# Sixteen hand-written orders of work, each replaced by another, in a gated mix of two recurrent attentions on one core

## The chip, the core and the metric

The kernel runs on one core of one Trainium2 chip. A core has five engines that work side by side, each through its own queue in order: TensorE (PE: matmuls; PEld is its loading of weights), VectorE (DVE), ScalarE (ACT), GpSimd (POOL) and SyncE (SP), which here only issues DMAs. Data lies in SBUF; matmuls write to PSUM, which the kernel uses as eight banks of 128 x 512 float32. The metric is device time in microseconds.

## The reference

`x` is [1, 2048, 512], all inputs bfloat16. Two branches read the same `x` and a gate per row mixes them:

```python
g = sigmoid((x * gate_w).sum(-1, keepdims=True))
return g * a + (1 - g) * b

# branch A: 64 segments of 32 tokens, one after the other; 8 rows of memory go from one to the next
mem = mem0                                           # [1, 8, 512]
for s in range(64):
    h = concatenate([mem, x[:, 32*s:32*s+32]], 1)    # 40 rows
    q, k, v = h @ Wq, h @ Wk, h @ Wv                 # 32 heads of 128: 512 -> 4096 each
    p = softmax(mask(q @ k.T * 128**-0.5))           # 40 x 40 for each head
    o = (p @ v) @ Wo                                 # 4096 -> 512
    mem = o[:, :8];  outs.append(o[:, 8:])

# branch B: 32 heads of 16, four stretches of 512 tokens
for s in range(4):
    a_dot = softmax(q_s @ k_s.T * 0.25 + causal) @ v_s
    a_mem = (phi(q_s) @ M) / (phi(q_s) @ z + 1e-6)   # phi(t) = t + 1 if t > 0 else exp(t)
    out_s = g_B * a_mem + (1 - g_B) * a_dot
    M, z = M + phi(k_s).T @ v_s, z + phi(k_s).sum(rows)
b = concat(out_s) @ wo
```

Branch A is a chain of 64 segments: the first rows of a segment's output are needed before the next segment's projections can begin.

## The kernel before

**Staging.** After some warming matmuls the kernel loads `x`, transposes it on TensorE (xT, features on partitions), and projects three of the four stretches of branch B (keys, queries and values, stored to DRAM scratch, and the sums M and z). The weights of branch A follow on SyncE's queue meanwhile. This takes to about 50 us and is not touched by the change. From there on, `plan_a` works off branch A's 64 segments in 16 groups of four, and the rest of branch B (its local attention, the projections of its fourth stretch, and the output rows) is strewn between.

**A segment.** Its 40 rows are 8 of memory and 32 of tokens. 32 rows (8 of memory and 24 of tokens, `hT`) go through the segment itself; the last 8 token rows of the four segments of a group are gathered into one set of 32 "left" rows (`xL`), which is projected once a group, ahead of its group. Four matmuls with 32 columns of weights each (`128*32`) stand side by side in the array, so a pass of 512 columns fills a whole bank.

**Who sets the order.** There is no scheduler. Each group has a list of unit names, written out in the source (`A_LIST0` to `A_LIST15`). `plan_a` reads it from left to right; each name records the instructions of one unit with what they read and write. Each engine executes its own instructions in the order recorded. The waits follow from the reads and writes: an engine waits at an instruction until what it needs has been done elsewhere. PSUM banks are given out in the same order (`Banks.take`, `give`), so a unit may also wait for the copy that frees its bank. SyncE's DMAs, too, stand in the recorded order, and one that waits holds up all behind it. The trace holds each engine's instructions in this order, so that each can be given its unit's name.

The names: `s.u` is unit u of segment s (0 to 3) of the group.
- `K0x K0y`, `Q1x` ...: a projection of one half of the heads (0, 1) in two half passes of eight matmuls each (L1305); `k0`, `q1`, `v0`: its copy from PSUM, on ScalarE (L390) or VectorE (L392); `TK0`, `TQ0`: the transpose on VectorE (L1317).
- `S0` scores (L1598, L1603), `X0` exp on ScalarE (L1612), `Y0` mask on VectorE (L1616), `M0` sums on TensorE (L1633), `L0` their reciprocal as ln and exp on ScalarE (L1640, L1643), `N0` the normalisation on VectorE (L1647), `n0` that of the left columns on GpSimd (L1653).
- `PV0` P times V (L1663), `PL0` the part with the left rows' values VL (L1675), `E0a E0b` the copies to OT, `W0a` ... four output passes (L1392).
- `H0`, `H1`: copies of the output's two halves to `WF` (L390 or L392); `F0`, `F1`: folds, small float32 matmuls that add the four strips and transpose (L1410); `hm0`, `hm1`: copies of the memory rows to the next segment's `hT`; `ax0`, `ax1`: of the other rows to `aT_st`. `oL`, `xc`, `qt` are copies on GpSimd.
- without a segment: `KL0x KL0 KL0e`, `QL..`, `VL..`: projection of the next group's left rows and its copies (with `i` in front: of group 0's own); once both halves of VL are copied they are stored to scratch (L1340, `scr_vld<-VNL`), and `VLt` loads them back in another arrangement (L1348, four DMAs `VL<-scr_vld`). `ol..`, `of`: the output of the left rows. `tl`, `tb`, `tf` (with `e`: their second part): the output rows of a finished group; `os` stores a group's rows.
- branch B: `bS` scores (L933), `bE` one exp of four (L954, `PT`, with a mask on GpSimd, L960), `bP` P times V (L986), `bT` the rest of a head group on VectorE (L1010 to L1046). `pj`, `pp`: a half pass of the fourth stretch's projections (L837) and its copy, which is followed by a store (L864; `t_sb` for the values). `wl`: one of eight loads of Wo (L552).
- `~` behind a name lets ScalarE and VectorE change places for the copies of this unit.

The functions that turn a name into instructions are the same in both kernels; a few lines fix what a name does with the engines:

```python
for u in ORDERS[g]:
    v.swap = u[-1] == "~"
    u = u.rstrip("~")
    if u in common:
        common[u]()
    elif u[0] in "0123":
        seg[int(u[0])][u[2:]]()
```

## Time and profile before

| | us |
|---|---|
| median of 3 runs | 836.16 (833.71 to 837.33) |
| the profiled execution's own time | 836.46 |
| its span, first to last instruction | 834.7 |
| TensorE busy in the span | 806.3 (97%) |
| ScalarE, VectorE, GpSimd busy | 597.6, 572.2, 285.3 |
| exps of branch B (L954), the largest group | 174.4, 320 of 0.607 |
| passes of 512 columns with Wq, Wk, Wv (L1305 on hT) | 138.3, 136.1, 138.7, 2048 matmuls each |

How to read it: the span lies inside the execution's own time, 1.8 us shorter. A matmul is counted from its start to its modelled end, some 0.38 us for 512 columns, while the next ones are already running; a matmul that starts late by less than that leaves no gap in the busy time. Times within the span are given from its start. The granted clock of TensorE is 1.000 over the span.

### The profile page before, as it was taken

The numbers are of one execution on the slowest core, as the hardware profiler recorded it, in microseconds if no ns is written. First come the engines' busy times: TensorE is split into PE (matmuls) and PEld (weight loads), VectorE is DVE, ScalarE is ACT, GpSimd is POOL, SyncE is SP. The second block draws the span as 40 slices with busy tenths as digits, with TensorE's granted clock in tenths as the row PEclk, the third lists the DMA queues.
The fourth block names the chain that finished last, engine by engine and source line by source line (L and its number), as shares of the span: only waits on it lengthen the run. The fifth ranks groups of instructions, "written<-read, shape, count | busy, mean of one in ns | idle before, by whom it ended". The sixth has DMA issues, their size and how long they took to land.

```text
span 834.7 us, 49033 instructions
## 1 busy us (share of the span) xinstructions
PE 806.3 (97%) x21947; PEld 433.9 (52%) x21947; DVE 572.2 (69%) x1379; ACT 597.6 (72%) x1523; POOL 285.3 (34%) x780
## 2 busy tenths in 40 slices
PE   9998999999999999999999999999999999999998
PEld 4644455555555555555555555554555554555544
DVE  4555565577677777777776776777776777777664
ACT  5546777777776777777677787777778676778645
POOL 3603242333333333334242333333333233434111
PEclk9999999999999999999999999999999999999999
DMA  8997312112111111111101121111112112110121
GB/s 327 418 370 224 81 32 67 42 32 47 33 30 40 31 48 29 44 39 46 36 20 40 36 56 26 46 39 34 36 32 53 22 37 46 44 38 5 29 60 41
DMA packets 98257, 57.48 MB, mean 69 GB/s; under 512 B 71800, under 2 KB 92160, under 8 KB 96512
## 3 DMA queue, kind: packets, MB, share of 16 engines
q1 hardware_dynamic: 97488, 53.58, 22.1%
q8 instruction: 172, 2.82, 1.4%
q10 hardware_dynamic: 560, 0.79, 0.3%
q14 instruction: 37, 0.30, 0.1%
HBM read 37.14 MB, written 17.20 MB: 65 GB/s over the span
## 4 chain that ended last, share of the span: by engine, by line
PE 82%; ACT 8%; DVE 4%; DMA 3%; issue 1%; SPq 1%; POOL 0%; ACTq 0%; DVEq 0%
PE ps L1305 45%; PE ps L1392 16%; PE ps L1410 3%; PE ps L1663 3%; PE ps L933 2%; PE ps L986 2%; DMA scr_kqd<-stgk 2%; PE ps L1598 1%; PE ps L699 1%; PE ps L1505 1%; PE ps L1633 1%; ACT PT L954 1%; ACT R_sb L1643 1%; ACT WF L390 1%; DVE P_sb L1647 1%
## 5 line engine op out<-in xcount | busy, mean ns | idle before, releaser
L960 POOL TENSOR_SCALAR_AFFINE_SELECT PT<-PT 128x128 bf16<-128x128 bf16 (+2 forms) x320 | 117.2, 366 | 197.4 <-ACT PT L954 156.8
L954 ACT ACTIVATE PT<-ps 128x512 bf16<-128x512 f32 x320 | 174.4, 607 | 3.8 <-PE ps L986 2.1
L1305 PE MATMUL ps<-Wq_sb,hT 128*32 128x512 bf16 x2048 | 138.3, 379 | 1.7 <-ACT PT L954 0.9
L1305 PE MATMUL ps<-Wv_sb,hT 128*32 128x512 bf16 x2048 | 138.7, 379 | 0.0
L1305 PE MATMUL ps<-Wk_sb,hT 128*32 128x512 bf16 x2048 | 136.1, 379 | 0.4
L1392 PE MATMUL ps<-Wo_sb,OT_sb 128*32 128x512 bf16 x2048 | 129.5, 380 | 0.7 <-ACT OT_sb L390 0.6
L1653 POOL TENSOR_TENSOR P_sb<-P_sb,R_sb 128x64 bf16<-128x64 bf16 x128 | 50.7, 396 | 145.3 <-ACT R_sb L1643 136.9
L390 ACT ACTIVATE OT_sb<-ps 128x320 bf16<-128x320 f32 x167 | 67.0, 434 | 24.2 <-PE ps L1675 22.9
L1305 PEld LDWEIGHTS ps<-Wq_sb,hT 128*32 128x32 bf16 x2048 | 58.7, 97 | 48.3 <-ACT hT L390 4.5
L1305 PEld LDWEIGHTS ps<-Wk_sb,hT 128*32 128x32 bf16 x2048 | 59.1, 97 | 45.4 <-ACT hT L390 2.1
L390 ACT ACTIVATE WF<-ps 128x256 f32<-128x256 f32 x108 | 36.2, 381 | 55.5 <-PE ps L1392 53.3
L1317 DVE STREAM_TRANSPOSE QT_sb<-QN_sb 128x256 f32<-128x256 f32 x128 | 56.2, 440 | 26.6 <-ACT QN_sb L390 24.3
L1317 DVE STREAM_TRANSPOSE KT_sb<-KN_sb 128x256 f32<-128x256 f32 x128 | 55.8, 438 | 24.6 <-ACT KN_sb L390 22.0
L390 ACT ACTIVATE QN_sb<-ps 128x512 bf16<-128x512 f32 x85 | 51.0, 600 | 29.8 <-PE ps L1305 28.5
L1392 PEld LDWEIGHTS ps<-Wo_sb,OT_sb 128*32 128x32 bf16 x2048 | 47.3, 96 | 46.0 <-ACT OT_sb L390 7.9
L390 ACT ACTIVATE KN_sb<-ps 128x512 bf16<-128x512 f32 x82 | 49.3, 601 | 29.2 <-PE ps L1305 28.7
L1305 PEld LDWEIGHTS ps<-Wv_sb,hT 128*32 128x32 bf16 x2048 | 50.4, 95 | 27.1 <-ACT QN_sb L390 0.7
L1612 ACT ACTIVATE P_sb<-ps 128x224 bf16<-128x224 f32 x128 | 45.8, 360 | 24.3 <-PE ps L1603 14.0
L1647 DVE TENSOR_TENSOR P_sb<-P_sb,R_sb 128x160 bf16<-128x160 bf16 x128 | 42.8, 335 | 22.4 <-ACT R_sb L1643 21.2
L392 DVE CAST OT_sb<-ps 128x320 bf16<-128x320 f32 x89 | 42.1, 487 | 19.0 <-PE ps L1675 18.1
L392 DVE CAST V_sb<-ps 128x512 bf16<-128x512 f32 x75 | 51.0, 681 | 4.2 <-PE ps L1305 2.5
L1663 PEld LDWEIGHTS ps<-P_sb,V_sb 32*128 32x128 bf16 x2048 | 23.2, 91 | 57.3 <-DVE P_sb L1647 21.8
(139 smaller groups left out, 1480.5 us busy)
## 6 DMA issues: line engine op xcount, KB each, us to landing
Wk_sb<-in_A_Wk_dram SPq DMA_DIRECT2D x4, 1024.0 KB, 10.2
Wq_sb<-in_A_Wq_dram SPq DMA_DIRECT2D x4, 1024.0 KB, 13.7
Wv_sb<-in_A_Wv_dram SPq DMA_DIRECT2D x4, 1024.0 KB, 16.0
Wo_sb<-in_A_Wo_dram SPq DMA_DIRECT2D x8, 512.0 KB, 5.3
scr_vld<-VNL SPq DMA_DIRECT2D x16, 256.0 KB, 3.3
VL<-scr_vld SPq DMA_DIRECT2D x64, 64.0 KB
scr_kqd<-stgk SPq DMA_DIRECT2D x12, 256.0 KB, 9.8
Vj<-scr_vd SPq DMA_DIRECT2D x32, 68.0 KB, 2.4
```

The source lines that it names most:

```text
L390: P.op("act", lambda a: a.activation(dst, src, ACT.Copy), reads=[v.rbank[k] for k in bks], writes=dres, name=name)
L392: P.op("dve", lambda d: d.tensor_copy(dst, src), reads=[v.rbank[k] for k in bks], writes=dres, name=name)
L954: P.op("act", lambda a: a.activation(pt, v.pb[bk], ACT.Exp, scale=v.SCALE_B), reads=[v.rbank[bk]], writes=[rp], name="be%d_%d" % (n, t))
L960: P.op("gp", lambda g: g.affine_select(mv, mv, [[0, len(cut)], [1, 128]], ALU.is_ge, 0.0, base=0, channel_multiplier=-1), reads=[rp], writ ...
L1305: ins = pe.matmul(pb[bk][SEG * j:SEG * (j + 1), :], lhs(c), cols(w, j) if split else w[:, 512 * j:512 * (j + 1)], start=(c == 0), stop=(c ...
L1317: P.op("dve", lambda d: d.transpose(to, src), reads=reads, writes=writes, name=name)
L1392: ins = pe.matmul(pb[bk][SEG * j:SEG * (j + 1), :], lhs(4 * k + j), Wo_sb[:, 4 * k + j, :], start=(first and k == ks[0]), stop=False, skip ...
L1410: ins = pe.matmul(pb[bk][SEG * j:SEG * (j + 1), SEG * n:SEG * (n + 1)], cols, v.fold[:, :], start=True, stop=True, skip_group_check=True)
L1612: P.op("act", lambda a: a.activation(P_sb[:, b, :], pb[bk][:, 0:224], ACT.Exp, scale=SCALE), reads=[rbank[bk]], writes=[Rs("P%d" % b), Rs( ...
L1647: P.op("dve", lambda d: d.tensor_tensor(wide(P_sb, b)[:, :, 0:L], wide(P_sb, b)[:, :, 0:L], R_sb[:, b, :].rearrange("p (i q) -> p i q", q= ...
L1653: P.op(ENG["n"], lambda d: d.tensor_tensor(left(P_sb), left(P_sb), grp04(R_sb[:, b, :]), ALU.mult), reads=[Rs("R%d" % b)], writes=[Rs("P%d ...
L1663: ins = pe.matmul(pb[bks[j]][:, L * i:L * (i + 1)], V_sb[SEG * j:SEG * (j + 1), b, i * E:(i + 1) * E], P_sb[SEG * j:SEG * (j + 1), b, LW * ...
```

## The change

All sixteen lists are replaced by other orders of the same units; nothing else is changed. Both kernels record 2337 groups of matmuls, 20667 matmuls, 776 instructions on GpSimd and 493 DMAs on SyncE. The places of `~` are other ones too: 1509 activations on ScalarE instead of 1522, and 485 copies on VectorE instead of 472. Of the copies to WF 31 instead of 20 are VectorE's. The instructions up to the last sums of branch B's third stretch, at 50 us, are the same, and then hardly two units in a row. The first list's beginning and the end of the last one, as a diff (lines left out of each list are marked):

```diff
 A_LIST0 = """
-    wl ixl iQL0x iKL0x 0.Q1x 0.Q1y iKL0 iKL0e~ wl iQL0 iQL0e~ 0.Q0x 0.Q0y iQL1x iQL1 0.K0x 0.K0y 0.k0 iQL1e pj 0.q1 wl iKL1x iKL1 iKL1e~ bS bE 0.V0x 0.q0
-    iVL0x 0.TQ0 0.V0y 0.V1x pj 0.V1y iVL0 0.TK0 pj pp 0.v1 bE 0.qt bE iVL0e~ pj bE iVL1x iVL1 xl bS iVL1e bP 0.xc bP QL0x bE bE 0.TQ1 0.v0 0.S0 wl 0.K1x
-    0.K1y KL1x bE wl 0.X0 0.Y0 bE KL1 pj pp 0.k1~ KL1e wl iVLt wl 0.TK1 0.M0 0.L0 QL0 bP wl QL0e bS 0.N0 bP bE VL0x VL0 0.S1 1.qt bE 0.X1 bE QL1x 0.Y1
-    VL0e QL1 pj pp QL1e~ 0.M1 0.L1 KL0x KL0 0.n0 0.n1 VL1x VL1 bE 0.PV0 0.PL0 0.N1 pj 0.E0a 0.E0b~ KL0e 0.PV1 0.PL1 0.E1b~ 0.E1a VL1e~ pj VLt 0.W0b 0.W0a
-    bP 0.W1a bP pp bT 0.W1b 0.H0 0.H1~ 1.xc bS 0.F0 bE 0.hm0 0.ax0 0.F1 0.hm1~ 1.K0x 0.oL bE 1.Q0x 1.K0y 1.k0~ 1.Q1x 1.Q1y 1.q1~ bE 1.TK0 1.Q0y bE 1.K1x
-    1.K1y bP bP 1.TQ1 1.q0~ 1.TQ0 1.V1x 1.S0 1.k1 1.TK1 1.X0 1.Y0 1.V0x 1.S1 1.X1 1.V0y 1.M0 1.V1y 1.L0 1.Y1 1.M1 1.L1 1.v0 1.n0 1.N0 1.PV0 1.PL0 1.n1
...
+    ixl wl 0.Q0x iKL0x iQL1x iQL0x 0.K0x 0.Q0y iQL0 0.K1x 0.K1y 0.q0 0.TQ0 iKL0 0.xc iQL0e 0.K0y iKL0e~ iKL1x 0.k1 bS wl bE bE bE iQL1 wl bE 0.k0~ iKL1 pj
+    iQL1e 0.qt 0.TK1 iVL1x iVL1 iVL0x iVL0 xl bP iVL0e pj bP iKL1e~ 0.TK0 0.Q1x iVL1e~ QL0x pp QL0 QL0e wl 0.Q1y bS VL0x wl bE VL0 0.V0x wl wl pj iVLt
+    0.q1~ bE 0.S0 bE pj KL1x 0.TQ1 bE 0.X0 0.Y0 0.S1 KL0x 0.X1 0.Y1 bP wl 0.V0y VL0e~ 0.M1 0.v0 bP 0.L1 0.N1 0.M0 KL1 KL0 pp VL1x VL1 KL1e KL0e~ bS 0.n1
+    pj pj 0.L0 0.N0 QL1x QL1 0.n0 VL1e~ bE bE 0.V1x 0.V1y bE QL1e bE 0.v1~ 0.PV0 1.qt 0.PL0 0.E0a 0.E0b~ 1.xc pj bP 0.PV1 0.PL1 0.E1a~ 0.W0b 0.E1b~ 0.W0a
+    0.oL 0.W1a bT 0.W1b pp 0.H0~ bP bS 0.F0 0.H1~ bE 0.hm0 0.ax0 pj 0.F1 0.hm1~ 1.Q0x 1.K0x 1.K0y bE bE 1.k0 0.ax1~ 1.TK0 1.Q0y 1.q0~ 1.TQ0 bE 1.K1x 1.K1y
+    1.Q1x 1.Q1y 1.k1 bP 1.TK1 1.S0 1.q1 1.TQ1 1.X0 1.Y0 1.V0x 1.V0y 1.v0 pp 1.S1 1.X1 1.Y1 1.M0 1.V1x 1.V1y 1.L0 1.n0 2.qt 1.N0 1.M1 1.L1 bP 1.n1 pj 1.v1
...
 A_LIST15 = """
...
-    2.H0 2.H1 2.F0 2.hm0 pl0 2.F1 2.hm1 3.K0x tfe 3.Q0x 2.ax0~ 3.Q0y 3.q0~ 3.K0y 3.k0 3.TQ0 3.K1x 3.K1y 3.Q1x tl 3.Q1y 3.TK0 3.S0 3.V0x 3.k1~ 3.q1 3.TK1
-    3.X0 3.TQ1 pl1x 3.V0y 3.Y0 3.S1 3.M0 2.ax1 3.X1 tb 3.v0 3.Y1 3.L0 3.n0 tbe 3.V1x 3.M1 tf 3.N0 tfe 3.L1 3.n1 3.N1 3.PV0 3.PL0 3.E0b~ 3.E0a 3.V1y 3.v1~
-    pl1 pl1e 3.W0a 3.PV1 3.PL1 3.W0b pf 3.E1b~ 3.W1b 3.E1a pfe~ 3.W1a 3.H0 3.H1 tl tb 3.F0 3.ax0 3.F1 3.ax1 tbe tf tfe
...
+    3.qt 2.F0 2.hm0 pl0 2.F1 3.Q0x 2.hm1~ 3.K0x 3.K0y tfe 3.Q0y 3.K1x 3.K1y 3.k0~ 3.TK0 3.Q1x 3.Q1y 3.q0~ 3.TQ0 2.ax1~ 3.S0 3.V0x 3.k1~ 3.TK1 3.q1 3.TQ1
+    3.V1x 3.V0y tl tf 3.S1 3.X0 3.Y0 3.X1 3.M0 tb 3.V1y 3.v0 3.L0 3.Y1 3.M1 3.N0 3.v1 2.ax0 tbe 3.L1 3.N1 tfe 3.n0 3.n1 3.PV0 3.PL0 3.E0b pl1x pl1 3.PV1
+    3.PL1 3.E1b 3.E0a 3.W0b 3.W0a 3.W1b 3.E1a pl1e 3.W1a 3.H0 pf pfe 3.H1 tl tb 3.F0 3.ax0~ 3.F1 tbe 3.ax1 tf tfe
     """
```

In group 0, for example, the old order begins with passes of the left rows and of Q1, has `bS` behind `0.K0y`, the four half passes of `iVL` spread over the units from `0.V0x` to `iVL1`, and `iVLt` behind the sixth `wl`; the new one begins with `0.Q0x`, has `bS` earlier, the four half passes of `iVL` in a row and `iVLt` behind the seventh `wl`. In the last group both end with the folds of segment 63, the left rows' output and the last output rows.

## The prediction

> **What bounds the kernel now.** I read the page first, then the table of stretches, then who TensorE waited for, and last the timeline of TensorE and of the DMA queue in the stretch after 50 us.

> ```profile
> span 834.7 us, 49033 instructions
> ...
> PE 806.3 (97%) x21947; PEld 433.9 (52%) x21947; DVE 572.2 (69%) x1379; ACT 597.6 (72%) x1523; POOL 285.3 (34%) x780
> ...
> PEclk9999999999999999999999999999999999999999
> ```

> TensorE is the bound from end to end, at the full granted clock; ScalarE and VectorE have a quarter of their time free. An order of units can only win or lose TensorE's waiting time. The table of stretches (span, TensorE, its weight loads, VectorE, ScalarE, GpSimd, clock, DMA share, GB/s) says where that is densest:

> ```profile
> 50.00:80.00 30.00, 26.15 (x597) 12.50 (x597) 16.64 (x36) 16.84 (x38) 7.55 (x21) 1.00 0.91 291
> 80.00:110.00 30.00, 28.51 (x816) 15.23 (x812) 17.65 (x44) 22.61 (x58) 9.39 (x27) 1.00 0.31 74
> 510.00:610.00 100.00, 98.88 (x2816) 51.89 (x2802) 74.34 (x179) 73.94 (x195) 35.21 (x90) 1.00 0.15 36
> ```

> From 50 to 80 us TensorE is idle 13% of the time, with the DMA engines 91% busy; later it is 1 to 3%. Its waits by releaser (total, times, longest):

> ```profile
> PE ps L1663 <- DVE P_sb L1647: 6.2, 16, 0.7
> PE ps L1410 <- ACT WF L390: 3.1, 13, 1.0
> ...
> PE ps L1675 <- DMA VL<-scr_vld: 1.2, 1, 1.2
> ```

> P times V waits for the normalisation (L1647), the folds wait for the copies of WF, and once the values of the left rows come late by DMA. These gaps count only what exceeds a matmul's own latency. A finer measure: the trace keeps the program's order, so each group of matmuls can be named by its unit, and the time from a group's start to the next can be set against the shortest usual one for that pair of kinds. A half pass of eight matmuls of 512 columns takes 0.43 us (50.49 to 50.92 on the timeline), scores 0.15, sums 0.10, P times V 0.10 plus 0.12, one fold 0.12; the step from a pass into P times V or into the local scores costs 0.54 instead of 0.43. So summed, all groups after 49.75 us need 727.2 us packed. The last group starts at 831.40, so 54.4 us are lost to waits: 5.3 up to the first pass of segment 1 at 79.75 us, and 49.1 in the 752 us behind it (0.78 a segment).

> The three largest early losses are on TensorE's timeline (start, length, group, idle time and its releaser):

> ```profile
> 62.84 0.40 PE L933 MATMUL ps<-QTj,KTj 32*128 32x256 bf16 x8 [0.89 <-ACT PT L954]
> ...
> 73.80 0.21 PE L1675 MATMUL ps<-P_sb,VL 32*128 32x64 bf16 x4 [1.16 <-DMA VL<-scr_vld]
> ...
> 79.07 0.33 PE L1410 MATMUL ps<-fold,WF 128*32 128x32 f32 x16 [1.00 <-ACT WF L390]
> ```

> and the DMA queue in front of the second:

> ```profile
> 62.72 0.34 SPq L1340 DMA_DIRECT2D scr_vld<-VNL  x1
> ...
> 66.52 0.34 SPq L864 DMA_DIRECT2D scr_vd<-t_sb  x1
> 66.90 0.44 SPq L552 DMA_DIRECT2D Wo_sb<-in_A_Wo_dram  x1
> 67.38 3.95 SPq L1348 DMA_DIRECT2D VL<-scr_vld  x4
> ```

> The store of the left values leaves at 62.72, the queue then stands behind the late store of 66.52, and the four loads need 3.95 us to be issued, so the last lands near 73.7.

> **The change, part by part.** Nothing is removed or added: 2337 matmul groups and 493 DMAs on SyncE's queue, before and after. 13 copies go from ScalarE to VectorE (about 13 x 0.6 = 8 us less on an engine busy 598 us, 13 x 0.7 = 9 more on one busy 572): free as load, since neither is the bound, and priced below where they stand on a path. *Packed sum:* 727.2 us again; the steps into P times V from something else go from 123 to 126 (3 x 0.11 = +0.3), into the local scores they stay 80. Cost nil.

> *Group 0 up to the first pass of segment 1.* Packed, this stretch is 24.7 us in both. I followed the new order by hand with durations of rows (copies 0.60 on ScalarE, 0.68 on VectorE, transposes 0.44, exp of the local attention every 0.48). Both start at 50.05.
> - The first local scores come earlier, packed at 55.3. They need a bank that the copy of KL0 frees, and it waits for the transpose of QL0, which VectorE reaches after the MZ product (ends 53.4), a copy and two transposes, at 55.0; the copy ends at 55.7. Wait 0.4.
> - The four half passes of VL0 end at 59.1 instead of 61.8, so their store leaves near 59.9, not 62.7. On the queue follow the first late store (60.9, as before: its copy waits for a memset that ended near 60.2) and four Wo loads of 0.46; the value loads need the store's landing, 59.9 + 3.3 = 63.2, then 3.95 to issue and 2.4 to land: 69.6. Their reader is packed at 71.2: the 1.3 us wait goes, with 1.6 us to spare. The last Wo load leaves at 67.5 and lands near 72.1 (72.5 and 77.1 before), ahead of its pass at 73.7.
> - The second local scores, packed at 61.6, need the late copy at 60.9: the 0.9 us wait goes.
> - Smaller: 0.15 at the third local scores (copy of KL1), 0.1 and 0.2 at the two P times V (exps and copies on ScalarE end at 71.1 and 72.1).
> - The first fold, 1.0 late before because the ScalarE copy of WF stood behind a late copy that waited for a store, now has its WF copy on VectorE, behind the chain of the local output (0.71 + 0.26 + 0.48): done at 75.0, 0.4 late.

> Waits 1.3 instead of 5.3: **-4.0 us**. Bounds: -5.3 if none is left, +0.8 if the landing goes wrong (a rival below).

> *The rest, 49.1 us of waits.* For each group that waits on another engine I took how much packed TensorE work lies between the last group that this engine had to see and the waiting group, and the mean loss at that distance in the trace of before; the new order has its own counts of such places:
> - fold 0: up to 0.35 us of cover 13 -> 12 (0.28 us lost each), to 0.55 8 -> 10 (0.11)
> - fold 1: up to 0.35 3 -> 5 (0.37), to 0.55 10 -> 5 (0.24), to 0.75 15 -> 18 (0.14)
> - first pass behind a fold: up to 0.13 17 -> 14 (0.24), to 0.35 11 -> 14 (0.20)
> - P times V: up to 0.35 6 -> 5 (0.56), to 0.72 15 -> 15 (0.12)
> - output pass behind its copy: up to 0.45 7 -> 5 (0.23)

> Together -1.3; with classes of 0.1 us the same count gives -2.8. I take **-1.5**, nearer the coarse one, whose classes hold more places. Each place scatters by about its mean: some 120 places by 0.25 us give 2.7 us for one order and 3.9 for the difference of two; that is the bound, from -5.4 to +2.4.

> *WF copies on VectorE.* The second half's go from 15 to 23, the first half's from 5 to 8. In the trace a fold 1 behind VectorE lost 0.16 us, behind ScalarE 0.09: 8 x 0.08 = +0.6; fold 0 lost 0.06 and 0.10: 3 x -0.05 = -0.1. **+0.5**. Queued behind such a copy on VectorE are the memory rows and the copies of the next K and Q; the fold, and through it the next segment, waits for it. Bounds: -0.5, and 11 x 1.1 = +12.1 if each stands behind one VectorE copy and one transpose (0.68 + 0.44).

> *Last group.* The last folds to the last transposition are packed the same (0.9 us); the load for output rows 14 is now nearer its reader, 1.8 instead of 3.6 us in the order, but the queue is free to issue it once the rows before have been stored, near 3 us ahead of VectorE's turn. Nil. *Row stores against the copies that reuse their tile:* within 5 us of cover 3 places before, one of which cost 0.4 us (465.59), and 3 after. Nil.

> **Sum:** -4.0 - 1.5 + 0.5 = -5.0, on the profiled execution's 836.46 (span 834.7 and 1.8 around it): **831.5 us**. The median of the runs shown, 836.16, is 0.3 lower than that execution; against it this is -0.56%.

> [...] The longest gap in TensorE's rows is 1.4 us (start to start at 72.37) and the granted clock is 1.00 in every stretch. [...]

> **The rivals.**
> - *The value loads land late all the same.* If the store takes as long to land as those to the same queue's scr_kqd (9.8 us median, with the DMA engines 91% busy as here), the loads are issued from 69.7 to 73.6 and land at 76.0, a wait of 4.8 us at L1675. The early gain turns to +0.8: 836.46 + 0.8 - 1.0 = 836.3. Against it: this very store had 3.3. It decides from a landing of about 5 us. [...] Chance 0.10.
> - *The early gain is given back later.* Early units pulled forward leave the rest as it was or up to 2.4 us worse, plus the 0.5: 836.46 - 4.0 + 2.9 = 835.4. For it: the packed sum and the counts are nearly the same. Chance 0.20.
> - *Slower: WF copies stand in VectorE's queue.* The segment's recurrence passes through WF, fold and memory rows; eleven more of its WF copies are VectorE's. If each waits for one copy and one transpose, +12.1: 836.46 - 4.0 + 12.1 = 844.6. From 0.4 us a boundary the change loses, from 0.7 by more than a measurement can tell. Against it: the 20 such copies of before lost 0.06 to 0.16 us each. Chance 0.15.

> **How the numbers follow.** Forecast 0.55, of which 0.46 lie under 832.0. What a measurement of this kernel can tell from no change is about 0.5%, 4.2 us: the three runs shown spread by 3.6. Faster by more than that 0.46; within it 0.09 + 0.20 + 0.10 = 0.39; slower 0.15. The range, from 827 (early waits gone entirely and most of the -5.4 behind them) to 838.5 (short of the slower case, past the late landing), leaves out some 0.05 below and 0.14 above.

> **What would show it.** In the profile after: no L1675 wait for VL at the first P times V, with the store of VNL near 60 us; the first fold near 75 us and the first pass of segment 1 near 75.8 instead of 79.75; TensorE busy about 27.5 of the 30 us from 50 to 80; the waits of L1663 on L1647 at or under 6.2 us, of L1410 on WF near 3. Wrong would be a first fold past 78 us, a wait for VL of more than 2 us, or more than 5 us of waits of L1410 on VectorE's WF.

## The result, and the profile after

The changed kernel takes 832.67 us (median of 22 executions, 829.88 to 836.26), the kernel before, beside it on the same chip, 835.46 us (22 executions, 833.61 to 838.33): a ratio of 0.9965, 95% interval 0.9952 to 0.9977. That is 2.8 us less, a real gain, but below the half per cent that was set as the bound for "faster". A second series, taken later, gave 0.9966 (0.9951 to 0.9980).

The profiled execution of the changed kernel took 830.58 us (span 828.9). Against the 836.46 us of the execution profiled before that is 5.9 us, twice what the medians differ by: one lies 2.1 us under its median, the other 1.0 over. So the two traces alone would overstate the gain.

From the page after, and its table of stretches (columns as before: stretch, span, TensorE, weight loads, VectorE, ScalarE, GpSimd, clock, DMA share, GB/s):

```profile
span 828.9 us, 49046 instructions
...
PE 804.7 (97%) x21947; PEld 433.6 (52%) x21947; DVE 575.6 (69%) x1392; ACT 592.2 (71%) x1510; POOL 287.6 (35%) x780
```

```profile
50.00:80.00 30.00, 26.91 (x626) 13.20 (x628) 16.27 (x38) 17.91 (x39) 8.53 (x23) 1.00 0.91 291
80.00:110.00 30.00, 28.95 (x832) 14.59 (x824) 19.69 (x48) 22.84 (x57) 8.58 (x25) 1.00 0.29 73
```

TensorE works 0.8 us more than before in the stretch from 50 to 80, where 1.35 more was forecast (27.5). Its waits after (total, times, longest):

```profile
PE ps L1663 <- DVE P_sb L1647: 2.9, 9, 0.7
PE ps L1410 <- ACT WF L390: 2.2, 11, 0.5
PE ps L1675 <- DMA VL<-scr_vld: 1.9, 1, 1.9
```

P times V and the folds wait less than before (6.2 and 3.1), but the wait on the left values, which was to go, has grown from 1.2 to 1.9 us. TensorE's timeline after shows the early losses:

```profile
55.93 0.40 PE L933 MATMUL ps<-QTj,KTj 32*128 32x256 bf16 x8 [0.56 <-ACT KN_sb L390]
68.76 0.40 PE L933 MATMUL ps<-QTj,KTj 32*128 32x128 bf16 x12 [0.52 <-ACT LN_sb L390]
73.97 0.21 PE L1675 MATMUL ps<-P_sb,VL 32*128 32x64 bf16 x4 [1.90 <-DMA VL<-scr_vld]
```

The chain of waits after, from 55 to 74 us (start, length, what), tells why the third line is there:

```profile
56.03 4.12 DMA scr_mzd<-MZ
...
60.24 0.70 DVE VNL L392
...
61.42 5.09 DMA scr_vld<-VNL
...
68.58 5.26 DMA VL<-scr_vld
...
73.97 0.21 PE ps L1675 x4
```

The half passes of VL0 ended at 59.5, as forecast (59.1). But the copies into VNL started at 60.24, when a store of MZ had landed. The code explains it: the helper that gives each tile the waits of the memory it reuses goes by the first letters of the name, and takes "VNL0" for a part of "VN", the values in V_sb, whose memory held MZ before. VNL has memory of its own. In the kernel before the copies came at 61.68, behind that landing, and the false wait cost nothing. The store then took 5.1 us to land, where 3.9 had been enough in the trace of before. The last value load landed 5.3 us after the start of its issue and 4.6 after the end; by the second count the trace of before has 2.3. Loads of Wo, of 512 KB each, stand close in front of both: three in front of the store, and four more in front of the value loads. The DMA engines are 91% busy from 50 to 80 us, in both traces.

By the same measure as in the prediction (start to start of the groups less the shortest usual step), TensorE loses 3.8 us instead of 5.3 up to the first pass of segment 1, and 45.1 instead of 49.4 behind it; the packed sums are equal (727.0).

### The profile page after: what moved, and what is told of

It reads as the page before. It is cut to its first block, busy times and chain, and to the rows that moved or that the text cites. A ratio compares the mean times of both kernels' runs of the same rounds, so it can differ in the third digit from the quotient of the medians.

```text
span 828.9 us, 49046 instructions
## 1 busy us (share of the span) xinstructions
PE 804.7 (97%) x21947; PEld 433.6 (52%) x21947; DVE 575.6 (69%) x1392; ACT 592.2 (71%) x1510; POOL 287.6 (35%) x780
## 4 chain that ended last, share of the span: by engine, by line
PE 81%; ACT 7%; DMA 5%; DVE 3%; issue 1%; POOL 1%; SPq 0%; ACTq 0%; DVEq 0%; POOLq 0%
PE ps L1305 44%; PE ps L1392 17%; PE ps L1410 4%; PE ps L1663 3%; PE ps L933 2%; PE ps L986 2%; DMA scr_mzd<-MZ 2%; PE ps L1505 2%; DMA scr_kqd<-stgk 2%; PE ps L1598 2%; PE ps L1633 1%; ACT PT L954 1%; PE ps L699 1%; ACT R_sb L1643 1%; ACT WF L390 1%
## 5 line engine op out<-in xcount | busy, mean ns | idle before, releaser
L954 ACT ACTIVATE PT<-ps 128x512 bf16<-128x512 f32 x320 | 176.1, 609 | 5.8 <-PE ps L933 3.9
L1392 PE MATMUL ps<-Wo_sb,OT_sb 128*32 128x512 bf16 x2048 | 127.4, 380 | 0.0
L390 ACT ACTIVATE OT_sb<-ps 128x320 bf16<-128x320 f32 x167 | 67.9, 434 | 22.8 <-PE ps L1675 21.7
L1392 PEld LDWEIGHTS ps<-Wo_sb,OT_sb 128*32 128x32 bf16 x2048 | 48.1, 96 | 45.7 <-ACT OT_sb L390 6.4
L390 ACT ACTIVATE QN_sb<-ps 128x512 bf16<-128x512 f32 x83 | 49.9, 602 | 28.4 <-PE ps L1305 27.5
L390 ACT ACTIVATE WF<-ps 128x256 f32<-128x256 f32 x97 | 32.8, 381 | 51.6 <-PE ps L1392 51.5
L390 ACT ACTIVATE KN_sb<-ps 128x512 bf16<-128x512 f32 x79 | 47.0, 599 | 25.7 <-PE ps L1305 24.8
L392 DVE CAST V_sb<-ps 128x512 bf16<-128x512 f32 x82 | 55.9, 683 | 4.0 <-PE ps L1305 3.1
L1647 DVE TENSOR_TENSOR P_sb<-P_sb,R_sb 128x160 bf16<-128x160 bf16 x128 | 42.2, 329 | 20.1 <-ACT R_sb L1643 18.4
L1663 PEld LDWEIGHTS ps<-P_sb,V_sb 32*128 32x128 bf16 x2048 | 23.0, 91 | 54.4 <-DVE P_sb L1647 27.9
```

The source lines that it names most:

```text
L390: P.op("act", lambda a: a.activation(dst, src, ACT.Copy), reads=[v.rbank[k] for k in bks], writes=dres, name=name)
L392: P.op("dve", lambda d: d.tensor_copy(dst, src), reads=[v.rbank[k] for k in bks], writes=dres, name=name)
L954: P.op("act", lambda a: a.activation(pt, v.pb[bk], ACT.Exp, scale=v.SCALE_B), reads=[v.rbank[bk]], writes=[rp], name="be%d_%d" % (n, t))
L1392: ins = pe.matmul(pb[bk][SEG * j:SEG * (j + 1), :], lhs(4 * k + j), Wo_sb[:, 4 * k + j, :], start=(first and k == ks[0]), stop=False, skip ...
L1647: P.op("dve", lambda d: d.tensor_tensor(wide(P_sb, b)[:, :, 0:L], wide(P_sb, b)[:, :, 0:L], R_sb[:, b, :].rearrange("p (i q) -> p i q", q= ...
L1663: ins = pe.matmul(pb[bks[j]][:, L * i:L * (i + 1)], V_sb[SEG * j:SEG * (j + 1), b, i * E:(i + 1) * E], P_sb[SEG * j:SEG * (j + 1), b, LW * ...
```

## The experiments

All ratios are to runs of the kernel before on the same chip, with 95% intervals.

**The first list alone, and the other fifteen alone.**

The first run, against the kernel before; the second changes the other fifteen lists in the same way and leaves list 0:

```diff
 A_LIST0 = """
-    wl ixl iQL0x iKL0x 0.Q1x 0.Q1y iKL0 iKL0e~ wl iQL0 iQL0e~ 0.Q0x 0.Q0y iQL1x iQL1 0.K0x 0.K0y 0.k0 iQL1e pj 0.q1 wl iKL1x iKL1 iKL1e~ bS bE 0.V0x 0.q0
+    ixl wl 0.Q0x iKL0x iQL1x iQL0x 0.K0x 0.Q0y iQL0 0.K1x 0.K1y 0.q0 0.TQ0 iKL0 0.xc iQL0e 0.K0y iKL0e~ iKL1x 0.k1 bS wl bE bE bE iQL1 wl bE 0.k0~ iKL1 pj
...
 A_LIST1 = """
-    0.K0x 0.Q0x bE bE 0.Q0y 0.q0 0.TQ0 0.K0y 0.k0 0.Q1x 0.Q1y 0.q1 0.TK0 0.qt 0.TQ1 0.K1x 0.K1y 0.k1 bP bP 0.S0 bT xl KL1x bS 0.X0 0.Y0 0.V0x 0.TK1 KL1
+    pp 0.K0x 0.Q0x bE bE 0.Q0y 0.q0 0.TQ0 0.K0y 0.k0 0.Q1x 0.Q1y 0.q1 0.TK0 0.qt 0.TQ1 0.K1x 0.K1y 0.k1 bP bP 0.S0 bT xl KL1x bS 0.X0 0.Y0 0.V0x 0.TK1 KL1
```

> The new list of group 0 with the old lists of groups 1 to 15 (one no-op finishing step is put ahead of list 1, so that the counts come out). Theory of the prediction: the early waits go, about 4.0 us less than the kernel before. Theory from the trace of the changed kernel: only 1.5 us are gained up to the first pass of segment 1 and 1.7 by the end of group 0, so 1.7 us less, with the wait for VL near 1.9 us in front of the first P times V as in the changed kernel. If the old lists behind it give the head start back: 0 to 0.5 us less.

> The old list of group 0 with the new lists of groups 1 to 15 (one finishing step left out of list 1, the counterpart of the run beside it). Theory of the prediction: -1.5 of waits and +0.5 for the WF copies, 1.0 us less than the kernel before. Theory from the two traces, whose lags behind group 0 differ by 4.1: 4.1 us less. Rival: what the two single traces show beyond the medians is scatter of executions, so 1.1 us less (2.8 in the medians, less 1.7 of group 0).

Measured: the first list alone 836.72 against 837.22, ratio 0.9996 (0.9981 to 1.0011); the rest alone 836.39, 0.9991 (0.9975 to 1.0007). Neither differs from no change; an early gain of 4.0 is excluded, and so is a gain of 4.1 in the rest. The two medians add up to 1.3 us less, the whole change to 2.8; the intervals are too wide to tell whether the two parts help each other. The trace of the first run shows something that none of the expectations had. Its timeline, and its table of stretches:

```profile
74.48 0.23 PE L1675 MATMUL ps<-P_sb,VL 32*128 32x64 bf16 x4 [2.48 <-DMA VL<-scr_vld]
...
76.13 2.79 PE L1392 MATMUL ps<-Wo_sb,OT_sb 128*32 128x512 bf16 x32
```

```profile
74.00:76.00 2.00, 1.52 (x40) 0.76 (x40) 0.49 (x1) 0.44 (x1) 0.00 (x0) 0.64 0.57 198
76.00:78.00 2.00, 2.00 (x40) 0.83 (x32) 1.68 (x4) 0.95 (x2) 0.40 (x1) 0.51 0.29 47
78.00:80.00 2.00, 1.90 (x60) 0.93 (x52) 0.93 (x3) 0.58 (x3) 0.00 (x0) 1.00 0.21 71
```

Behind the wait of 2.5 us the granted clock is at one half, from 74.55 to 77.97 us, and the 32 matmuls of the output passes take 2.79 us where the changed kernel's profiled run, at full clock, took 1.91. The first pass of segment 1 starts at 80.17, at a loss of 5.3 us, as large as before the change. So the longer wait and the clock take back the early gain. Every execution reports its mean granted clock, this profiled one 0.998 over its span: one such stretch takes 0.002 from the mean (half of 3.4 us in 835.4). Ten of the 12 executions of the first run had 0.998 or less, one of the 12 of the second.

**VNL without the false wait.**

```diff
     def late_home(name):
-        if name.startswith(("aTd", "aTg", "PT")):
+        if name.startswith(("aTd", "aTg", "PT", "VNL")):
             return None
```

> The changed kernel, and the tile VNL no longer inherits the waits of V_sb, whose memory it does not share: its copies need not wait until the store of MZ has landed. Theory that this wait is why the early gain is 1.5 and not 4.0: the copies start near 59.2 instead of 60.2, their store leaves near 60.0 instead of 61.4, the Wo loads behind it end 1.4 earlier too, the value loads are issued from 65.1 instead of 66.5, the wait of the first P times V on VL falls from 1.9 to about 0.5 us, and the kernel gains 1.0 to 1.4 us on the changed one. Rival, that the landing is set by the crowded DMA engines: VL lands near 73.9 all the same, wait 1.7 to 1.9, no gain. Second rival: the wait goes but the time is lost at the next late step before segment 1 (first fold still near 77), under 0.4 us gained.

Measured: 833.69, ratio 0.9958 (0.9943 to 0.9972). The copies start at 58.82 and 59.55, the store leaves at 60.74, the loads from 65.64, VL is read at 73.16 instead of 73.97. The false wait was real, and it was worth 0.8 us of landing. The wait on VL is 1.7 (TensorE also arrives 0.5 earlier), the loss up to segment 1 is 2.7 us. The gain of the ratio over the changed kernel, 0.0007, is inside the intervals. So the false wait is a part of the lateness; the rest lies behind the store's issue, with 4.9 us to that of the loads and 7.5 more until VL is read.

**The WF copies on their old engines, in the new order; and the new engines in the old order.**

The first run, at 14 such places, and the second line at 3 such places (list 14 is shown):

```diff
-    0.oL 0.W1a bT 0.W1b pp 0.H0~ bP bS 0.F0 0.H1~ bE 0.hm0 0.ax0 pj 0.F1 0.hm1~ 1.Q0x 1.K0x 1.K0y bE bE 1.k0 0.ax1~ 1.TK0 1.Q0y 1.q0~ 1.TQ0 bE 1.K1x 1.K1y
+    0.oL 0.W1a bT 0.W1b pp 0.H0 bP bS 0.F0 0.H1~ bE 0.hm0 0.ax0 pj 0.F1 0.hm1~ 1.Q0x 1.K0x 1.K0y bE bE 1.k0 0.ax1~ 1.TK0 1.Q0y 1.q0~ 1.TQ0 bE 1.K1x 1.K1y
...
-    2.L1 2.PV0 2.PL0 2.v1 2.E0b 2.E0a~ 2.N1 QL0 ol0x 2.PV1 2.n1 2.PL1 2.W0a 2.W0b 2.E1a~ 2.W1a 2.E1b~ 2.W1b ol0 VLt bP 2.H0 bP QL0e~ 2.F0 2.H1 2.hm0 ol1x
+    2.L1 2.PV0 2.PL0 2.v1 2.E0b 2.E0a~ 2.N1 QL0 ol0x 2.PV1 2.n1 2.PL1 2.W0a 2.W0b 2.E1a~ 2.W1a 2.E1b~ 2.W1b ol0 VLt bP 2.H0~ bP QL0e~ 2.F0 2.H1 2.hm0 ol1x
```

The second run makes the reverse changes in the lists of before.

> The changed kernel with every copy of WF on the engine that it had before (14 marks taken out, 3 put back: 11 copies from VectorE to ScalarE), the order as changed. Theory of the prediction: these copies cost 0.5 us, so 0.5 us less than the changed kernel. Rival, that they stand in VectorE's queue: up to 12 us less. Rival, that they are a part of the gain (the waits of folds fell from 13.3 to 12.3 us in the traces): 0.5 to 1.5 us more than the changed kernel.

> The old order in all groups with the new marks of the WF copies (14 to VectorE, 3 to ScalarE). Theory that these copies are a gain by themselves, as the run with the old marks in the new order says: 2.5 to 3.0 us less than the kernel before. Theory of the prediction: 0.5 us more. Third: a mark is worth something only in the order that it was searched with, so 0 here, up to 2 us more.

Measured: the new order with the old marks takes 837.56, ratio 0.9999 (0.9983 to 1.0015): the gain of the change is gone. Against the changed kernel that is 3.4 us more, where at most 1.5 was expected. The old order with the new marks takes 842.37, ratio 1.0062 (1.0046 to 1.0078): 5.3 us slower, far outside all three expectations. The marks are neither good nor bad in themselves: their worth is that of the order around them. In the trace of the first, three folds carry most of the cost: 0.93 us at segment 50, 0.55 at 58, 0.43 at 55; over all 17 places the folds lose 2.0 us more than in the changed kernel, whose losses at these folds differ by no more than some 0.01 us between five traces. Where the other 1.4 us lie stays open. In the trace of the second the same 17 folds lose 4.5 us more than before. TensorE's waits there, and its timeline:

```profile
PE ps L1410 <- DVE WF L392: 3.2, 5, 1.4
```

```profile
744.59 0.33 PE L1410 MATMUL ps<-fold,WF 128*32 128x32 f32 x16 [1.40 <-DVE WF L392]
```

VectorE's timeline in front of that fold:

```profile
742.78 0.49 DVE L392 CAST aT_st<-ps 128x64 bf16<-128x64 f32 x2 [1.35 <-PE ps L1410]
743.19 0.28 DVE L1003 TENSOR_SCALAR pQj<-pQj 128x512 bf16<-128x512 bf16 x1
743.50 0.69 DVE L1004 SCALAR_TENSOR_TENSOR pQj<-QTj,pQj 128x512 bf16<-128x512 bf16 x1
744.11 0.74 DVE L392 COPY WF<-ps 128x256 f32<-128x256 f32 x2
```

The copy of WF stands behind work of 1.3 us that has nothing to do with it. That is the mechanism of the slower rival, in the old order; in the new order, with the same engine, this fold (segment 55) loses 0.06 us.

**Two of these copies alone.** Segment 50's second half and segment 58's first go back to VectorE.

Beside the line of list 14 shown above, this one of list 12:

```diff
-    2.v1~ 2.PV0 2.PL0 2.E0a bP bP QL0 2.E0b~ QL0e~ 2.PV1 2.PL1 2.E1a 2.E1b~ 2.W0a 2.W0b bT 2.W1a 2.oL 2.W1b 2.H0 bS ol0x 2.F0 2.hm0~ 2.ax0~ 2.H1 2.F1 bT
+    2.v1~ 2.PV0 2.PL0 2.E0a bP bP QL0 2.E0b~ QL0e~ 2.PV1 2.PL1 2.E1a 2.E1b~ 2.W0a 2.W0b bT 2.W1a 2.oL 2.W1b 2.H0 bS ol0x 2.F0 2.hm0~ 2.ax0~ 2.H1~ 2.F1 bT
```

> The changed kernel with two copies of WF put back on VectorE (segment 50 second half, segment 58 first half; both went from VectorE to ScalarE in the change). In the trace with all the old marks these two folds lose 0.93 and 0.65 us where the changed kernel loses 0.00 and 0.10. Theory that the cost sits in these places and is the same whatever the rest does: the same losses here, 0.9 and 0.6, and none at the other folds. Rival, that it comes from the sum of the marks: losses spread, these two under 0.3.

Measured: the two folds lose 0.93 and 0.65 us, the others what they lose in the changed kernel (segment 55: 0.06, segment 53: 0.06). The time, 833.30, is one execution and says little. The reading of places holds: a wait at a fold belongs to the order and the engine there.

VectorE's timeline in the run with all the old marks shows the first of the two:

```profile
678.52 0.17 DVE L392 CAST hT<-ps 128x16 bf16<-128x16 f32 x1 [0.54 <-PE ps L1410]
678.62 0.20 DVE L392 CAST aT_st<-ps 128x48 bf16<-128x48 f32 x1
678.73 0.41 DVE L392 COPY WF<-ps 128x256 f32<-128x256 f32 x1
```

The second half's copy of WF stands behind the memory rows of the first half, which wait for the first half's fold. On ScalarE, in the changed kernel's trace, both halves' copies run from 672.95 to 673.61, ahead of the memory rows at 673.98 and 674.14, and this fold loses 0.00 us.

**The clock: once more the changed kernel, and a longer gap.** In the second run the value loads go behind the last Wo load and the late store.

```diff
-    iQL1e 0.qt 0.TK1 iVL1x iVL1 iVL0x iVL0 xl bP iVL0e pj bP iKL1e~ 0.TK0 0.Q1x iVL1e~ QL0x pp QL0 QL0e wl 0.Q1y bS VL0x wl bE VL0 0.V0x wl wl pj iVLt
+    iQL1e 0.qt 0.TK1 iVL1x iVL1 iVL0x iVL0 xl bP iVL0e pj bP iKL1e~ 0.TK0 0.Q1x iVL1e~ QL0x pp QL0 QL0e wl 0.Q1y bS VL0x wl bE VL0 0.V0x wl wl pj
...
-    0.q1~ bE 0.S0 bE pj KL1x 0.TQ1 bE 0.X0 0.Y0 0.S1 KL0x 0.X1 0.Y1 bP wl 0.V0y VL0e~ 0.M1 0.v0 bP 0.L1 0.N1 0.M0 KL1 KL0 pp VL1x VL1 KL1e KL0e~ bS 0.n1
+    0.q1~ bE 0.S0 bE pj KL1x 0.TQ1 bE 0.X0 0.Y0 0.S1 KL0x 0.X1 0.Y1 bP wl 0.V0y VL0e~ 0.M1 0.v0 bP 0.L1 0.N1 0.M0 KL1 KL0 pp iVLt VL1x VL1 KL1e KL0e~ bS 0.n1
```

> The changed kernel once more, on the chip of the three runs beside it. Theory: the wait of the first P times V on VL (1.9 to 2.5 us in the traces so far) lowers the granted clock of TensorE in some executions: means of 0.996 to 0.998 over the span in more than half of them and 1.000 in the rest, with 1.5 to 2 us between the two groups; the kernel before has such executions in about a quarter. Rival: the clock has nothing to do with this change, and the shares are equal.

> The changed kernel with the four value loads put behind the last Wo load and the late store, about 2.5 us later on the queue. Theory that a longer gap of TensorE always lowers its clock: wait on VL 4 to 5 us, mean clock 0.998 or lower in every execution, passes of about 0.8 us instead of 0.43 behind the gap, and the kernel 3.0 to 4.5 us slower than the changed one (2.5 of wait and the clock). Rival, that the clock has nothing to do with it: 2.0 to 2.5 us slower, the shares of lowered executions as in the changed kernel.

Measured: the changed kernel 834.19 against 837.05, ratio 0.9966 (0.9951 to 0.9980); six of 12 executions with a mean clock of 0.998 or less. Its trace is one of these, with the clock at one half from 74.67 to 78.08 after a wait of 2.2 us. The later loads: 837.56, ratio 0.9999 (0.9981 to 1.0017), 3.4 us above the changed kernel; 11 of 12 executions lowered, six of them to 0.996. Its wait on VL is 4.8 us, and the clock stays at one half for twice as long, 74.57 to 81.39:

```profile
74.00:76.00 2.00, 0.00 (x0) 0.00 (x0) 0.00 (x0) 0.00 (x0) 0.00 (x0) 0.64 0.51 175
76.00:78.00 2.00, 1.61 (x40) 0.84 (x40) 0.49 (x1) 0.44 (x1) 0.00 (x0) 0.50 0.02 7
78.00:80.00 2.00, 2.00 (x32) 0.79 (x24) 1.75 (x4) 0.96 (x2) 0.40 (x1) 0.50 0.27 41
80.00:82.00 2.00, 2.00 (x32) 0.71 (x24) 0.45 (x3) 0.00 (x0) 0.00 (x0) 0.65 0.21 72
```

**The loads earlier.** VNL free, and the value loads two Wo loads ahead; then one.

The first added line is the first run's, the second the second's:

```diff
-    iQL1e 0.qt 0.TK1 iVL1x iVL1 iVL0x iVL0 xl bP iVL0e pj bP iKL1e~ 0.TK0 0.Q1x iVL1e~ QL0x pp QL0 QL0e wl 0.Q1y bS VL0x wl bE VL0 0.V0x wl wl pj iVLt
+    iQL1e 0.qt 0.TK1 iVL1x iVL1 iVL0x iVL0 xl bP iVL0e pj bP iKL1e~ 0.TK0 0.Q1x iVL1e~ QL0x pp QL0 QL0e wl 0.Q1y bS VL0x wl bE VL0 0.V0x pj iVLt wl wl
+    iQL1e 0.qt 0.TK1 iVL1x iVL1 iVL0x iVL0 xl bP iVL0e pj bP iKL1e~ 0.TK0 0.Q1x iVL1e~ QL0x pp QL0 QL0e wl 0.Q1y bS VL0x wl bE VL0 0.V0x wl pj iVLt wl
```

> The changed kernel without VNL's false wait, and the four value loads put two Wo loads (512 KB each) ahead of their place on SyncE's queue. Theory that the Wo transfers ahead of them set the landing and the landing sets the early loss: VL is there before the first P times V (wait 0 to 0.4 us instead of 1.9), the first pass of segment 1 starts near 76.0, the granted clock is 1.000 in nearly all executions, and the kernel gains 2.0 to 3.0 us on the changed one (1.9 of the wait, the rest of the clock). Rival, that the Wo loads behind are now late: a wait of the output passes (L1392) of 1 to 3 us, gain under 0.5 us.

> The changed kernel, VNL without its false wait, and the value loads one Wo load ahead of their place (with two ahead, the wait for VL was gone and one of 1.5 us for the last Wo loads stood in its place). Theory that the DMA engines, busy to 76 us, hand out a fixed lateness, and that the clock is lost where it falls on TensorE in one piece: two waits of 0.4 to 1.1 us, on VL and on Wo, the first pass of segment 1 near 77.3 as with VNL freed alone, a mean clock of 0.998 or less in a quarter of the executions at most, and a ratio to the kernel before near 0.994. Rival: the share stays at a half and the ratio between 0.9955 and 0.997, as in the runs with VNL freed and with the loads two ahead.

Measured, two ahead: 834.19, ratio 0.9968 (0.9947 to 0.9989), six of 12 executions lowered. VL is there, and the output pass waits instead. Its timeline:

```profile
72.11 0.21 PE L1675 MATMUL ps<-P_sb,VL 32*128 32x64 bf16 x4
...
76.39 0.61 PE L1392 MATMUL ps<-Wo_sb,OT_sb 128*32 128x512 bf16 x8 [1.49 <-DMA Wo_sb<-in_A_Wo_dram]
```

The rival was right. The loss up to segment 1 is 3.8 us, that of the changed kernel's first trace. One ahead: 833.40 against 837.31, ratio 0.9950 (0.9930 to 0.9969), the best of all, one of 6 executions lowered. Its two waits:

```profile
72.41 0.21 PE L1675 MATMUL ps<-P_sb,VL 32*128 32x64 bf16 x4 [0.43 <-DMA VL<-scr_vld]
...
75.34 0.61 PE L1392 MATMUL ps<-Wo_sb,OT_sb 128*32 128x512 bf16 x8 [0.37 <-DMA Wo_sb<-in_A_Wo_dram]
```

First pass of segment 1 at 77.19, loss 2.8 us. The lateness is cut in two pieces of 0.4 us. Its interval overlaps that of the changed kernel, so that it beats the kernel before is shown (by 0.3 to 0.7%), that it beats the changed one is only likely.

**The gap filled with work.** 24 matmuls whose result is overwritten stand ahead of the first P times V, once in the changed kernel, once with VNL free.

```diff
+            def f_fill(pe):
+                ins = None
+                for n in range(24):
+                    c, j = n // 4 % 4, n % 4
+                    ins = pe.matmul(pb[bks[0]][SEG * j:SEG * (j + 1), :], lhs(c), Wv_sb[:, c, 512 * j:512 * (j + 1)],
+                                    start=True, stop=True, skip_group_check=True)
+                return ins
+            if s == 0 and b == 0:
+                P.op("pe", f_fill, reads=rx(0) + rx(1) + [Rs("Wv")], writes=[rbank[bks[0]]], name="fz")
```

> The changed kernel with 24 more matmuls of 512 columns (1.3 us, results overwritten) ahead of the first P times V, so that TensorE is busy in the first 1.3 us of its wait for VL; nothing waits for them. Theory that the gap lowers the clock: the gap shrinks from 1.9 to 0.6-0.9 us, the share of executions with a mean clock of 0.998 or less falls from 20 in 34 to a quarter or less, and the median falls by 0.8 to 1.3 us against the changed kernel (ratio to the kernel before near 0.995). Rival, that the clock falls for another reason in that place: the same share and the same time as the changed kernel (0.9965), or up to 1.3 us more where VL came early.

> The same 24 matmuls, and VNL without its false wait. Theory: the gap is 0.4 us or nothing, the clock stays at 1.000 in nearly all executions, 0.7 to 1.0 us less than the run with the matmuls alone (ratio near 0.994). Rival: no better than VNL freed alone (0.9958).

Measured: waits on VL of 1.3 and 0.8 us; lowered executions 1 of 6 and 1 of 12. The kernel before had 10 of 17 on this chip and 22 of 74 on the two others, so the small share is not the chip's: in these runs the share of lowered executions follows the gap (2 of 18 here, 20 of 34 of the changed kernel at 1.9 and 2.2 us). The times did not follow: 834.25, ratio 0.9962 (0.9946 to 0.9977), and 834.39, 0.9966 (0.9954 to 0.9978), where 0.995 and 0.994 were expected. With the 24 matmuls alone VL is read at 74.21, between the 73.97 and 74.41 of the changed kernel's two traces, so no cost of theirs shows at that place; with VNL free as well it is read at 73.54, against 73.16 without them. Gaps that no engine explains (see the last section) come to 2.4 and 3.2 us in these two traces, against 0.9 in the changed kernel's first, but they range from 0.3 to 2.9 in the other traces of the new order; whether that is where the expected 1 us went stays open.

The clock in one table, with the wait on VL in the trace (for two ahead, that on Wo) and the executions at a mean clock of 0.998 or less. A wait is that of one traced execution, a count is over all, and the chips differ:

| kernel | wait, us | lowered |
|---|---|---|
| VL late | 4.8 | 11 of 12 |
| first list alone | 2.5 | 10 of 12 |
| two old marks | 2.4 | 0 of 1 |
| changed, two series | 1.9, 2.2 | 20 of 34 |
| old marks | 1.9 | 7 of 12 |
| VNL free | 1.7 | 7 of 12 |
| two Wo loads ahead | 1.5 | 6 of 12 |
| before, four series | 1.2 | 32 of 91 |
| filled, filled with VNL free | 1.3, 0.8 | 2 of 18 |
| one Wo load ahead | 0.4 | 1 of 6 |

Of the kernel before, executions with a lowered clock took 839.0 us on average and the others 836.8 (8 lowered and 25 at 1.000, of the first series): 2.2 us between them, with 1.2 to 3.1 in the other series that have several of both. Relative to before, the changed kernel has it in 24 more of 100 executions, so some 0.5 us of its gain goes to the clock, an estimate. "The rest alone" (1 of 12) and "old order, new marks" (1 of 6) have the early list of before and fewer lowered executions than it, which may be chance in so few.

## Why the prediction was right or wrong

The time forecast, 831.5, is 1.2 us under the median and the range held it. That it is so near is in part luck: the gain was put at 5.0 us and measured at 2.8, and the execution that the forecast starts from lay 1.0 us above the median of the longer series. The forecast of "faster by over 0.5%" did not come true: the gain is 0.35%. By its steps:

- *Group 0 up to the first pass of segment 1, "-4.0 us"*: this step failed. The profiled run gained 1.5 us at full clock, and other executions nothing (losses of 5.3 to 5.7 in the three traces of this list with a lowered clock, 5.3 before). The sub-step that failed is "the 1.3 us wait goes, with 1.6 us to spare". The half passes ended near the forecast (59.5), but the store left at 61.42 instead of 59.9, 0.7 us of it for a false wait that I overlooked because it cost nothing in the trace of before (without it the store left at 60.74). It landed after 5.1 us instead of 3.3, and the last load 4.6 us after the end of its issue instead of 2.4. The 3.3 was misread: it is the median of the kernel's sixteen such stores, and "this very store" took 3.9 in the trace of before. The 2.4 comes from a row with six Wo loads in front instead of seven. The issue of the four loads, put at 3.95 us, took 2.7, which gave 1.2 us back. First fold 77.50 instead of 75.0, first pass 78.21 instead of 75.8. Of the small steps the first bS wait (0.56, forecast 0.4), the second, gone, and the first fold, without a wait, went about as forecast; the third bS wait was 0.52 instead of 0.15.
- *The value-load rival (0.10)* was the one that came true in its mechanism: the landing of the store was put at 5 us as the point where it decides, and it was 5.1. Its price was too high (4.8 us of wait; it was 1.9 to 2.5). By the prediction's own signs of being wrong, a first fold past 78 us and a wait for VL of more than 2, the changed kernel's first trace is just inside (77.50 and 1.90) and its second outside (79.44 and 2.2). The forecast's own sum had no term for the clock, which was lowered in 20 of 34 executions of the changed kernel: behind waits of 1.94, 2.16 and 2.48 us it was at one half for 3.4 us, and at a wait of 4.8 us, which the rival names, in the run with the late loads, for 6.8 us.
- *The rest, "-1.5"*, and *the WF copies, "+0.5"*: together -1.0 forecast. Behind the first pass of segment 1 the trace of before loses 49.4 us (and that of its lists 1 to 15 behind the new first one 49.7); five traces of the changed order (the changed kernel twice, VNL free, the loads two and one ahead) lose 45.1 to 47.6. But the late loads and the two filled runs, which differ from them in group 0 alone, lose 49.6, 47.2 and 48.6, and the new fifteen lists behind the old first one lose 49.4. So the term was a gain of some 0 to 4 us in single traces, and the run of these fifteen lists alone (0.8 us less, interval from 2.1 less to 0.6 more) does not contradict the 1.0 that was forecast: whether the term was mis-sized stays open. The copies had the wrong sign: at their folds the new marks save 2.0 us in the new order. I priced them by the mean loss behind VectorE (0.06 to 0.16 us). A mean has no meaning here: in either order 11 or more of the 17 places lose within 0.3 us of each other on the two engines, and a few lose 0.4 to 1.5 us on the wrong one.
- *The slower rival (WF copies in VectorE's queue)* did not happen in this order, and does with these marks in the old one (+5.3 us; 1.40 us in one fold, where 1.1 was put).
- The waits of L1663 on L1647 (2.9, forecast at or under 6.2) and of L1410 on WF (2.2, near 3) went as forecast.

In the first two traces an early gain that was put 2.5 us too high and a later one that was put 3.3 too low offset each other; in the changed kernel's second trace the early gain is gone (a loss of 5.7) and the later one is 3.3. So the nearness of the total says little for the steps.

## What to carry to other kernels

Before a transfer is moved forward, look at every wait of its chain, also those that cost nothing now, and at the bytes on the queue in front of it: a landing time read from a row holds for the traffic in that row only, and a median over many rows is not the row (the store here took 3.9 us before and 5.1 after, where the median of its kind is 3.3). Where a fixed amount of data is late, share the lateness between its readers: in pieces of 0.43 and 0.37 us it left one of 6 executions with a lowered clock here, while the four traces with 1.94 us or more of idle TensorE in one of the clock's stretches all had it, and such executions were some 2 us longer (1.2 to 3.1). A choice of engine for one copy is priced by what stands in front of it at that place in that order, not by a mean over the others.

## What the runs showed that was not expected

The falls go with TensorE's idle time within one stretch of the grid, the 3.41 us between two of its points. The four stretches that end in a fall hold 1.94, 2.16, 2.48 and 3.01 us of it; of those at full clock that do not, none holds more than 1.66; behind one of 1.82 at half clock it stayed there, in the run with the late loads. So in these traces stretches with a fall and those without part somewhere between 1.66 and 1.94 us. The wait of 1.90 us in the changed kernel's first trace was cut by the grid at 72.87 into 0.80 and 1.10, and the clock stayed up. The run with two old marks had a longer wait than two of the four that were lowered, cut at 73.11 into 1.63 and 0.79, and its clock stayed up as well:

```profile
73.91 0.21 PE L1675 MATMUL ps<-P_sb,VL 32*128 32x64 bf16 x4 [2.42 <-DMA VL<-scr_vld]
```

If the place of the grid is left to chance, and 1.7 to 1.9 us in one stretch are taken to be enough, a wait of 1.9 us brings that much into one stretch in 44 to 56% of the executions, an estimate from these figures; 20 of 34 were counted. The trace of the kernel before has no 3.41 us behind 8 us with more than 1.33 idle, so its 32 of 91 stay unexplained.

*In most of the traces TensorE stalls at the same places of its instruction stream.* Some gaps that no engine explains ("issue") lie inside a group of matmuls. TensorE's timeline of the kernel before, of the changed kernel, and of the changed kernel with 24 matmuls more:

```profile
691.81 0.19 PE L1410 MATMUL ps<-fold,WF 128*32 128x32 f32 x1 [0.63 <-issue]
```

```profile
686.92 0.19 PE L1410 MATMUL ps<-fold,WF 128*32 128x32 f32 x1 [0.94 <-issue]
```

```profile
688.53 0.23 PE L1410 MATMUL ps<-fold,WF 128*32 128x32 f32 x3 [0.81 <-issue]
```

Counted from the start of the program, each stands in front of matmul 18018. The 24 more did not move the stall with the work: it went 24 matmuls up in the program, from the sixteenth matmul of one fold into the fold before. This place is in most of the traces, give or take two matmuls, with 0.8 to 1.4 us from start to start; others are 7333 and 15348, each in more than half of the traces, with 0.3 to 1.2. Not every execution stalls at every place, and reordering the units did not remove them. The traces show what these places have in common. The page lists a queue `q8 instruction` of 172 packets, 16 KB each, one to some 127 matmuls. In the 14 traces 42 gaps of over 0.2 us behind matmul 3000 are put down to "issue". All 42 end 1.2 to 1.6 us after the end of such a packet; of all matmuls only one in eleven starts so. The last packet ahead of matmul 18018 is the 141st in every trace. Whether TensorE waits there for what these packets bring was not shown: no run changed them.
